# Six PSUM score banks as one tile with dependencies written out, and two subtractions of the row maximum in place of four

## The chip, the cores and the metric

The kernel runs on one core of a Trainium2 chip. Times are microseconds (us) of device time for one execution; the metric is the median of several executions. Engines: PE is TensorE (matmuls), PEld its weight load, DVE is VectorE, ACT is ScalarE, POOL is GpSimd, SP issues most DMAs. PSUM, where matmuls write, has eight banks of 512 float32 columns on 128 partitions.

## The reference, cut to what matters

Attention over pooled keys, followed by a soft mixture of experts. Keys and values are the same 768 pooled and projected rows a batch; there are 4 batches of 12288 queries of 128 channels.

```python
def _attn_ref(q, kv, w_sr):
    ...
    kv_pool = kv.reshape(B, H // r, r, W // r, r, C).mean(axis=(2, 4))
    kv_flat = kv_pool.reshape(B, -1, C) @ w_sr
    k = v = kv_flat
    s = scale * (q @ k.transpose(0, 2, 1))
    s = s - s.max(-1, keepdims=True)
    a = np.exp(s)
    a /= a.sum(-1, keepdims=True) + 1e-09
    return (a @ v).astype(np.float32)

def _moe_ref(x, phi, w1, w2):
    logits = x @ phi
    d = np.exp(logits - logits.max(0, keepdims=True)); d /= d.sum(0, keepdims=True) + 1e-09
    slot_input = d.T @ x
    ...
    c = np.exp(logits - logits.max(1, keepdims=True)); c /= c.sum(1, keepdims=True) + 1e-09
    return (c @ slot_out).astype(np.float32)
```

## The kernel before, in words

The queries are worked on in 96 blocks of 512. A block's scores are 6 tiles of 128 keys by 512 queries, one PSUM bank each, so six banks hold one block; the other two (`m0`, `m1`) serve everything else. The six are three PSUM tiles of two banks, with the tags s0, s1 and s2, allocated anew for every block.

For block i the steps are these. `qk(i, t)` (L553) makes score tile t with three matmuls, L560 to L562, high and low parts of keys and queries. `rowmax1` (L574) takes maxima over 32-query squares of two banks at once on DVE (L578); `rowmax2` (L588, L590) combines them, one small matmul on PE (`rowmax_pe`, L598) spreads them over the partitions, `rowmax3` (L603) reduces that and `rowmax4` (L608) transposes it into `mb`. `sub(i, t, n)` (L611) subtracts `mb` from n banks and writes to SBUF, into one of two tiles of three banks a block (L616). With a pair of banks a tile, four subtractions cover the six banks: banks 0 and 1, bank 2, bank 3, banks 4 and 5 (L1209). ACT makes two exponentials of each half (L624, L628), POOL their difference (`plo`, L633), and PE multiplies both parts by the values: `av_hi` (L650, L651) and `av_lo` (L658), four quarters of 128 queries a block. Every fourth block, a group of 2048 queries is worked into the experts' sums (`group_ops`, L1035), which adds smaller operations on all engines. The tail behind the last block runs the experts and writes the output; it uses the same six banks in pairs.

The order on PE, DVE, ACT and POOL is written out by the kernel's own planner (`Plan`, L37). Each operation has an engine, an assumed cost, a priority, operations that it depends on, and keys of buffer rings that it acquires or uses. The planner plays the program through with these costs and emits the instructions engine by engine in the order that results; the chip then runs each engine in that order. A ring entry is free again when its last user is done plus 0.08 us. A subtraction of n columns is assumed to cost n / 960 + 0.07 us. A block's first score matmul acquires ring s0, its third s1 and its fifth s2; the subtractions are among the users. For blocks below AHD = 10 the high part of the attention output may run before the low part of the exponentials is there; from block 10 on, its first piece also depends on `los`, POOL's low parts (L1164).

```python
for t, n in ((0, 2), (2, 1), (3, 1), (4, 2)):
    h, o2 = divmod(t, TH)
    ops["s", i, t] = op("DVE", dve(n * BQ), 0.08, ...)
```

Semaphores are set by the framework from the tiles that instructions touch. The first matmul into a newly allocated pair waits for the release of the pair's previous tile, that is for its last readers on DVE and for PE's own last writes.

Of the kernel before, what the change touches and what calls it, by code (L numbers as in the profile page):

```python
# [9 lines left out]
F32 = mybir.dt.float32  # L10
# [26 lines left out]
class Plan:  # L37
# [22 lines left out]
    def emit(self):  # L60
# [105 lines left out]
        while todo:  # L166
# [36 lines left out]
            fn()  # L203
        self.end = max(done)
# [3 lines left out]
def attention_then_soft_moe(ctx: ExitStack, tc: tile.TileContext, qT, kv0, kvT, w_sr, w_srT, phi, w1, w2, outT):  # L208
# [35 lines left out]
    TBUF = 3  # L244

# [66 lines left out]
    S = {}  # L312
# [9 lines left out]
    NU = NT // 2  # L322
# [3 lines left out]
        "pooled": 1, "v32": 1, "r6": 2, "rq": 2, "m1": 2, "mb": 1, **{f"s{u}": 1 for u in range(NU)},  # L326
# [3 lines left out]
    banks = [pm.tile([P, 512], F32, tag=f"m{b}", name=f"m{b}") for b in range(2)]  # L330

# [16 lines left out]
    WARM = (("s2", 2.2, 30, 0.32, 20.0), ("m", 26.3, 30, 0.22, 46.0))  # L348
# [215 lines left out]
    def qk0_hi(t):  # L564
        khi = kT[0][0]
        S[0, t // 2] = ps.tile([P, 2, BQ], F32, tag=f"s{t // 2}", name=f"s_0_{t // 2}")
        for u in range(2):
            for k in range(2):
                nc.tensor.matmul(S[0, t // 2][:, u, :], khi[:, (t + u) * P : (t + u + 1) * P], qsp[0][k], start=(k == 0), stop=False)

    def qk0_lo(t):
        nc.tensor.matmul(S[0, t // 2][:, t % 2, :], kT[0][1][:, t * P : (t + 1) * P], qsp[0][0], start=False, stop=True)

    def rowmax1(i, t, n):  # L574
        if t == 0:
            MX[i] = sp.tile([P, NT, NBK], F32, tag="r6", name=f"r6_{i}")
        u = t % 2
        nc.vector.tensor_reduce(  # L578
            out=MX[i][:, t : t + n, :].rearrange("p t b -> p (t b)"),
            in_=S[i, t // 2][:, u : u + n, :].rearrange("p t (b j) -> p (t b) j", j=Q32), axis=X,  # L580
# [30 lines left out]
    def sub(i, t, n):  # L611
        h, o = divmod(t, TH)
        if o == 0:
            TT_[i, h] = sp.tile([P, TH, BQ], F32, tag="t", name=f"t_{i}_{h}", bufs=TBUF)
        u = t % 2
        nc.vector.tensor_tensor(  # L616
            out=TT_[i, h][:, o : o + n, :], in0=S[i, t // 2][:, u : u + n, :],
# [18 lines left out]
    def av_tile(i, k):  # L636
        if k % 2 == 0 and i == NB - 1:
            PX[i, k // 2] = ps.tile([P, 2, BQ], F32, tag=f"s{k // 2}", name=f"px_{i}_{k}")[:, :, :VW]
# [323 lines left out]
    def warm(n, ring):  # L962
        if ring == "m":
            t = mt([P, 512], f"wm_{n}")
        elif n in W0:
            t = W0[n]
        else:
            t = W0[n] = ps.tile([P, 2, BQ], F32, tag=ring, name=f"wm_{n}")[:, 0, :]
# [145 lines left out]
    def av_rest(i, k, m, p, prev):  # L1114
        los = [ops["lo", i, 0], ops["lo", i, 1]]
        a2 = end_lo = op("PE", 6 * 0.072, 0.17, p + 0.8, prev + los, lambda: av_lo(i, k), use=[("plo", (i, 0)), ("plo", (i, 1)), m])
        if k % 2:
# [3 lines left out]
            if i == NB - 1:  # L1121
                v = k // 2
                q = HEAD + (i - 2) * PER + 0.01 * v
                a2 = op("DVE", 0.16, 0.08, q, [a2], lambda: l_x(v), use=[m], raw=0.05)
                a2 = op("DVE", 0.16, 0.08, q, [a2], lambda: l_r(v), raw=0.05)
                a2 = ops["l", v] = op("DVE", 0.24, 0.08, q, [a2], lambda: l_l(v), use=[m], raw=0.05)
            ops["x", i, k // 2] = op(
                "DVE" if i == NB - 2 and k == 1 else "ACT", act(2 * VW) + (0.1 if i == NB - 2 and k == 1 else -0.03), 0.1, p - 2, [a2] + evs[-1:], lambda: av_evac(i, k // 2),
                acq=[x] if first else [], use=[m] + ([] if first else [x]),
# [7 lines left out]
    def av_ops(i):  # L1137
# [7 lines left out]
        px = [(f"s{k // 2}" if end else "m", ("px", i, k // 2)) for k in range(TB)]  # L1145
        base = prev
        for k in range(TB if i < AHD else 0):
# [5 lines left out]
            for t in range(0, NT, AVS):  # L1153
                prev = [op("PE", 2 * AVS * 0.0702, 0.17, p, prev, lambda i=i, k=k, t=t: av_hi(i, k, t), acq=[m] if k % 2 == t == 0 else [], use=pp + ([m] if k % 2 or t else []))]
# [5 lines left out]
        for k in range(TB if i >= AHD else 0):  # L1160
            m = px[k]
            p = T0 + AVD * PER + 1.3 * k
            for t in range(0, NT, AVS):
                a1 = op("PE", 2 * AVS * 0.0702, 0.17, p, prev + ([] if end or t else los), lambda i=i, k=k, t=t: av_hi(i, k, t), acq=[m] if k % 2 == t == 0 else [], use=pp + ([m] if k % 2 or t else []))  # L1164
# [13 lines left out]
    for i in range(NB):  # L1178
# [8 lines left out]
        for t in range(NT):  # L1187
            u = t // 2
            if i == 0 and t == NT - 2:
                hi2 = op("PE", 4 * 0.2315, 0.0, T0 - QKP + 0.65 * t, [ops["ql", 0], ops["kh", 2], ops["qk", 0, t - 1]], lambda: qk0_hi(NT - 2), acq=[(f"s{u}", 0)], use=[("qs", 0)], raw=0.0)  # L1190
            ops["qk", i, t] = op(
                "PE", 0.2315, 0.17, T0 - QKP + 0.65 * t, [hi2] + kd + ([ops["qk", 0, t - 1]] if t == NT - 1 else []), lambda t=t: qk0_lo(t), use=[("qs", 0), (f"s{u}", 0)], raw=0.0,
# [407 lines left out]
```

## Time and profile before

| | before |
|---|---|
| median of 3 runs | 1063.73 us (1063.14 to 1064.67) |
| profiled execution, first to last instruction (its span; no other time of its own is listed) | 1063.4 us |
| PE busy | 1028.3 us, 97% |
| DVE busy | 972.7 us, 91% |
| POOL busy | 870.1 us, 82% |
| ACT busy | 794.1 us, 75% |
| DVE, row maxima L578 | 354.1 us, 289 instructions |
| DVE, subtractions L616 | 342.0 us, 384 instructions |
| mean granted TensorE clock | 0.990 |

An engine's busy time is the union of its instructions' spans. Matmuls overlap in the pipeline, so a matmul of 0.23 us may start 0.07 us behind the one before. A view of waits names the instruction that waited, what ended the wait, the total, how often, and the longest. A timeline lists instructions in order of start; neighbours of a kind are merged with a count (x2), the duration then reaching from the first start to the last end.

### The profile page before, as it was taken

To read this page: it belongs to the slowest core of one execution; us is meant where nothing else is said; L and a number is where in the kernel's file an instruction comes from. 1 tells how busy PE (TensorE), PEld (TensorE's weight loads), DVE (VectorE), ACT (ScalarE), POOL (GpSimd) and SP (SyncE) were. 2 spreads that over 40 slices of the span, in tenths; PEclk is the share of its full clock that TensorE was granted. 3 is DMA by queue.
4 is the path that set the end of the run, shared out by engine and by line. 5 is a ranking of instruction groups with operands and counts; after the bars stand their busy time and mean duration, and the time that the engine had idled before them with its cause. 6 is when DMAs were issued, how large, how long until landed. Compare 5 with 4: busy or idle time off the path is not lost.

```text
span 1063.4 us, 24815 instructions
## 1 busy us (share of the span) xinstructions
PE 1028.3 (97%) x10250; PEld 881.3 (83%) x10250; DVE 972.7 (91%) x1556; ACT 794.1 (75%) x1046; POOL 870.1 (82%) x505
## 2 busy tenths in 40 slices
PE   8999999999999999999999999999999999999894
PEld 5788888888888888988888888988888888888452
DVE  6989999999999999999999999999999999998684
ACT  3777787788777787788787787788787777776473
POOL 0789998889989989889989988889889999893800
PEclk9999999999999999999999999999999999999898
DMA  9234410120136320120146310120110110113598
GB/s 370 110 87 88 116 56 1 42 96 6 41 85 134 71 57 1 41 100 2 41 104 116 86 41 1 41 100 1 41 41 2 41 41 2 41 41 96 206 398 370
DMA packets 15729, 89.17 MB, mean 84 GB/s; under 512 B 1664, under 2 KB 1920, under 8 KB 9344
## 3 DMA queue, kind: packets, MB, share of 16 engines
q1 hardware_dynamic: 11728, 69.47, 17.6%
q0 software_dynamic: 3312, 17.70, 8.8%
q8 instruction: 81, 1.33, 0.5%
q10 hardware_dynamic: 576, 0.41, 0.1%
q14 instruction: 32, 0.26, 0.1%
HBM read 58.87 MB, written 25.17 MB: 79 GB/s over the span
## 4 chain that ended last, share of the span: by engine, by line
PE 87%; DVE 8%; DMA 3%; ACT 1%; issue 1%; POOL 0%; SPq 0%; DVEq 0%; ACTq 0%
PE m L650 15%; PE m L658 14%; PE m L651 14%; PE s L560 12%; PE s L562 11%; PE s L561 11%; PE m L831 2%; DVE r L578 2%; DVE t L616 2%; PE po L1429 2%; DMA outT<-o 2%; PE m L1401 1%; PE m L1407 1%; DMA kv<-kv 1%; DVE m L603 1%
## 5 line engine op out<-in xcount | busy, mean ns | idle before, releaser
L633 POOL TENSOR_TENSOR plo<-t,phi 128x1536 f16<-128x1536 f32 x190 | 599.2, 3164 | 93.1 <-ACT t L628 84.2
L624 ACT ACTIVATE phi<-t 128x1536 f16<-128x1536 f32 x192 | 283.5, 1478 | 148.1 <-DVE t L616 148.1
L578 DVE TRANSPOSE_TENSOR_REDUCE r<-s 128x32 f32<-128x1024 f32 x289 | 354.1, 1234 | 8.3 <-PE s L562 1.6
L650 PE MATMUL m<-vhi,phi 128*128 128x161 f16 x2280 | 353.2, 234 | 8.1 <-DVE m L603 7.3
L651 PE MATMUL m<-vlo,phi 128*128 128x160 f16 x2280 | 352.4, 233 | 0.0
L616 DVE TENSOR_TENSOR t<-s,mb 128x1024 f32<-128x1024 f32 (+1 forms) x384 | 342.0, 950 | 6.2
L628 ACT ACTIVATE t<-t 128x1536 f32<-128x1536 f32 x192 | 283.1, 1476 | 1.2
L650 PEld LDWEIGHTS <-phi 128*128 128x128 f16 x2304 | 224.1, 98 | 21.7 <-issue 21.5
L560 PE MATMUL s<-qhi,khi 128*128 128x512 f32 x574 | 237.1, 413 | 0.6 <-DVE t L616 0.4
L651 PEld LDWEIGHTS <-phi 128*128 128x128 f16 x2304 | 225.1, 98 | 12.1 <-issue 10.6
L562 PE MATMUL s<-qhi,klo 128*128 128x512 f32 x574 | 224.6, 391 | 0.0
L561 PE MATMUL s<-qlo,khi 128*128 128x512 f32 x574 | 223.9, 390 | 0.0
L658 PE MATMUL m<-vhi,plo 128*128 128x161 f16 x2280 | 223.5, 234 | 0.0
L658 PEld LDWEIGHTS <-plo 128*128 128x128 f16 x2304 | 171.9, 98 | 2.8 <-issue 2.7
L550 POOL TENSOR_TENSOR qlo<-q,qhi 128x512 fp32r<-128x512 f32 x95 | 127.9, 1346 | 23.9 <-ACT qhi L545 23.9
L562 PEld LDWEIGHTS s<-qhi,klo 128*128 128x128 f32 x574 | 107.7, 188 | 23.8
L560 PEld LDWEIGHTS s<-qhi,khi 128*128 128x128 f32 x574 | 107.9, 188 | 21.8 <-issue 2.6
L561 PEld LDWEIGHTS s<-qlo,khi 128*128 128x128 f32 x574 | 108.2, 189 | 19.4 <-issue 0.7
L668 ACT ACTIVATE xl<-m 128x322 f32<-128x322 f32 x189 | 81.4, 431 | 50.3 <-PE m L658 43.7
L608 DVE STREAM_TRANSPOSE mb<-m 128x512 f32<-128x512 f32 x96 | 68.3, 711 | 3.3
L545 ACT ACTIVATE qhi<-q 128x512 fp32r<-128x512 f32 x96 | 59.5, 620 | 2.8 <-DMA q<-qT 2.8
L603 DVE TENSOR_REDUCE m<-m 128x16 f32<-128x64 f32 x96 | 21.5, 224 | 22.8 <-PE m L598 19.1
(196 smaller groups left out, 843.3 us busy)
## 6 DMA issues: line engine op xcount, KB each, us to landing
q<-qT SPq DMA_DIRECT2D x23, 1024.0 KB, 5.0
outT<-o SPq DMA_DIRECT2D x22, 1024.0 KB, 7.6
kva<-kvT POOLq DMA_DIRECT2D x9, 1536.0 KB, 11.7
kva<-kvT SPq DMA_DIRECT2D x3, 1536.0 KB, 12.8
kv<-kv SPq DMA_DIRECT2D x6, 512.0 KB, 6.1
w<-w SPq DMA_DIRECT2D x2, 1536.0 KB, 6.4
w<-w SPq DMA_DIRECT2D x4, 768.0 KB, 4.2
kva<-kva POOLq DMA_DIRECT2D x3, 768.0 KB, 10.6
```

Source lines behind the costliest of these rows:

```text
L550: eng.tensor_tensor(out=lo, in0=q_src(i), in1=hi.bitcast(F32), op=ALU.subtract)
L560: nc.tensor.matmul(s, khi[:, ks], hi, start=True, stop=False)
L561: nc.tensor.matmul(s, khi[:, ks], lo, start=False, stop=False)
L562: nc.tensor.matmul(s, klo[:, ks], hi, start=False, stop=True)
L578: nc.vector.tensor_reduce(out=MX[i][:, t : t + n, :].rearrange("p t b -> p (t b)"), in_=S[i, t // 2][:, u : u + n, :].rearrange("p t (b j) ...
L616: nc.vector.tensor_tensor(out=TT_[i, h][:, o : o + n, :], in0=S[i, t // 2][:, u : u + n, :], in1=MX[i].unsqueeze(1).broadcast_to([P, n, BQ ...
L624: nc.scalar.activation(hi, TT_[i, h], AF.Exp, scale=SCALE)
L628: nc.scalar.activation(t, t, AF.Exp, scale=SCALE)
L633: eng.tensor_tensor(out=lo, in0=TT_.pop((i, h)), in1=PP[i, h][0], op=ALU.subtract)
L650: nc.tensor.matmul(px, p, vhi[:, t, :], start=(t == 0 and (i >= AHD or k % 2 == 0)), stop=False)
L651: nc.tensor.matmul(px[:, 1:], p, vlo[:, t, :], start=False, stop=False)
L658: nc.tensor.matmul(px, PP[i, t // TH][1][:, t % TH, ks], vhi[:, t, :], start=False, stop=(t == NT - 1 and (i >= AHD or k % 2 == 1)))
```

## The change

The three pair tiles become one PSUM tile `SB` of six banks that lives for the whole program. For the framework's tracking of this tile, a hook that runs after every planned operation puts orders between instructions on different engines bank by bank: an instruction waits, of the instructions on other engines that touched `SB`, only for the last one on each of its own banks (and for those that share another tensor with it). In the planner, the three rings of pairs become six rings of one bank; score tile t acquires ring t alone, and users of pairs name both banks. The subtraction runs over three banks at a time. The rest is renaming: the warm-up's bank, the last block's output, and the tail use slices of `SB`.

```diff
+    SUBS = ((0, 3), (3, 3))
...
-        "pooled": 1, ..., **{f"s{u}": 1 for u in range(NU)},
+        "pooled": 1, ..., **{f"s{t}": 1 for t in range(NT)},
...
+    SB = ps.tile([P, NT, BQ], F32, tag="s", name="s")
...
+    def order_banks():
+        for inst in seen:
+            if inst.opcode == "Ldweights":
+                continue
+            mine = banks_of(inst.outs) | banks_of(inst.ins)
+            if not mine:
+                continue
+            need = {x.name: x for b in mine for e, x in HELD.setdefault(b, {}).items() if e != inst.engine}
+            beside = others_of(inst)
+            for e, tensors in users.items():
+                if e != inst.engine:
+                    tc.declare_no_dep(
+                        inst, group=f"S{e}", keep=[x for x in need.values() if x.engine == e] + [x for n in beside for x in tensors.get(n, ())], reason="banks are waited for one by one"
+                    )
+            for n in beside:
+                users.setdefault(inst.engine, {}).setdefault(n, []).append(inst)
+            for n in need:
+                tc.add_manual_dep(inst, n, mybir.DependencyInfo(mybir.DependencyClass.Sync, mybir.DependencyReason.DATA), reason="same bank")
+            tc.add_to_no_dep_group(f"S{inst.engine}", inst)
+            for b in mine:
+                HELD[b][inst.engine] = inst
+        seen.clear()
...
     def qk(i, t):
-        if t % 2 == 0:
-            S[i, t // 2] = ps.tile([P, 2, BQ], F32, tag=f"s{t // 2}", name=f"s_{i}_{t // 2}")
-        s = S[i, t // 2][:, t % 2, :]
+        s = SB[:, t, :]
...
     def sub(i, t, n):
-        u = t % 2
         nc.vector.tensor_tensor(
-            out=TT_[i, h][:, o : o + n, :], in0=S[i, t // 2][:, u : u + n, :],
+            out=TT_[i, h][:, o : o + n, :], in0=SB[:, t : t + n, :],
...
-                lambda i=i, t=t: qk(i, t), acq=[(f"s{u}", i)] if t % 2 == 0 else [], use=[("qs", i)] + ([(f"s{u}", i)] if t % 2 else []),
+                lambda i=i, t=t: qk(i, t), acq=[(f"s{t}", i)], use=[("qs", i)],
...
-        for t, n in ((0, 2), (2, 1), (3, 1), (4, 2)):
+        for t, n in SUBS:
...
-                acq=[("t", (i, h))] if o2 == 0 else [], use=[(f"s{t // 2}", i), ("mb", i)] + ([("t", (i, h))] if o2 else []),
+                acq=[("t", (i, h))] if o2 == 0 else [], use=[(f"s{x}", i) for x in range(t, t + n)] + [("mb", i)] + ([("t", (i, h))] if o2 else []),
...
-    plan.emit()
+    nc.push_inst_callback(note)
+    plan.emit(order_banks)
+    nc.pop_inst_callback()
```

## Rows read from the trace of the kernel before

**Rows 1.** Busy us by engine, sum of the four 200 us stretches from 60 to 860:

```profile
sum 800.00, PE 791.74 PEld 700.24 DVE 758.09 ACT 629.50 POOL 721.83; mean PE 197.94 PEld 175.06 DVE 189.52 ACT 157.37 POOL 180.46
```

**Rows 2.** Who waited for whom: us in total, times, longest us:

```profile
ACT phi L624 <- DVE t L616: 148.1, 89, 2.8
...
DVE m L603 <- PE m L598: 19.1, 34, 0.9
...
PE m L650 <- DVE m L603: 7.3, 23, 0.3
```

**Rows 3.** Timeline of DVE, one block: start, duration, line, operation:

```profile
280.30 0.22 DVE L603 TENSOR_REDUCE m<-m 128x16 f32<-128x64 f32 x1
280.55 0.71 DVE L608 STREAM_TRANSPOSE mb<-m 128x512 f32<-128x512 f32 x1
...
281.30 1.22 DVE L616 TENSOR_TENSOR t<-s,mb 128x1024 f32<-128x1024 f32 x1
...
282.44 1.28 DVE L616 TENSOR_TENSOR t<-s,mb 128x512 f32<-128x512 f32 x2
...
283.04 1.81 DVE L616 TENSOR_TENSOR t<-s,mb 128x512 f32<-128x512 f32 x2
```

**Rows 4.** Timeline of PE and its weight loads, the same block:

```profile
280.06 0.20 PE L598 MATMUL m<-rq,sel_h 128*128 128x64 f16 x1
280.10 0.59 PE L658 MATMUL m<-vhi,plo 128*128 128x161 f16 x6
280.57 0.23 PE L650 MATMUL m<-vhi,phi 128*128 128x161 f16 x1
...
283.05 0.19 PEld L560 LDWEIGHTS s<-qhi,khi 128*128 128x128 f32 x1
```

**Rows 5.** Groups by shape on DVE: subtractions, busy us and mean ns:

```profile
L616 DVE TENSOR_TENSOR t<-s,mb 128x1024 f32<-128x1024 f32 x192 | 234.1, 1219 | 6.2
L616 DVE TENSOR_TENSOR t<-s,mb 128x512 f32<-128x512 f32 x192 | 123.1, 680 | 0.0
```

**Rows 6.** Timeline, second block's first weight load behind a subtraction:

```profile
27.99 1.22 DVE L616 TENSOR_TENSOR t<-s,mb 128x1024 f32<-128x1024 f32 x1
...
29.27 0.19 PEld L560 LDWEIGHTS s<-qhi,khi 128*128 128x128 f32 x1 [0.40 <-DVE t L616]
```

**Rows 7.** Timeline, an early block: subtraction, last matmul, weight load:

```profile
74.75 1.23 DVE L616 TENSOR_TENSOR t<-s,mb 128x1024 f32<-128x1024 f32 x1
...
75.84 0.23 PE L651 MATMUL m<-vlo,phi 128*128 128x160 f16 x1
...
76.12 0.47 PE L560 MATMUL s<-qhi,khi 128*128 128x512 f32 x1
...
76.09 0.19 PEld L560 LDWEIGHTS s<-qhi,khi 128*128 128x128 f32 x1 [0.23 <-issue]
```

**Rows 8.** Instructions of line L560: duration ns min/median/max, first and last start:

```profile
L560 PEldq EVENT_SEMAPHORE  x282: 51/51/51, 30.5 to 957.3; - x141
```

**Rows 9.** First subtraction and next score weight load: first and last of 46, then of 29:

```profile
131.55 1.22 DVE L616 TENSOR_TENSOR t<-s,mb 128x1024 f32<-128x1024 f32 x1
133.30 0.19 PEld L560 LDWEIGHTS s<-qhi,khi 128*128 128x128 f32 x1
...
943.51 1.22 DVE L616 TENSOR_TENSOR t<-s,mb 128x1024 f32<-128x1024 f32 x1
945.25 0.19 PEld L560 LDWEIGHTS s<-qhi,khi 128*128 128x128 f32 x1
...
122.21 1.23 DVE L616 TENSOR_TENSOR t<-s,mb 128x1024 f32<-128x1024 f32 x1
123.88 0.19 PEld L560 LDWEIGHTS s<-qhi,khi 128*128 128x128 f32 x1
...
952.93 1.23 DVE L616 TENSOR_TENSOR t<-s,mb 128x1024 f32<-128x1024 f32 x1
954.61 0.19 PEld L560 LDWEIGHTS s<-qhi,khi 128*128 128x128 f32 x1
```

More of the change, by code (lines that the diff above doesn't have):

```diff
@@ L58, in op, with emit @@
         return n
-    def emit(self):
+    def emit(self, after):
         ops = self.ops
@@ L203, in emit @@
             fn()
+            after()
         self.end = max(done)
@@ L311, in attention_then_soft_moe @@
     qsp = {}
-    S = {}
     MX = {}
@@ L321, in attention_then_soft_moe @@
     NBK = BQ // Q32
-    NU = NT // 2
     plan = Plan({
         "m": 2, "t": TBUF, "phi": PB, "plo": PB, "q": 2, "qs": 2, "xl": 2, "D": 1, "kv": 2,
-        "pooled": 1, "v32": 1, "r6": 2, "rq": 2, "m1": 2, "mb": 1, **{f"s{u}": 1 for u in range(NU)},
+        "pooled": 1, "v32": 1, "r6": 2, "rq": 2, "m1": 2, "mb": 1, **{f"s{t}": 1 for t in range(NT)},
     })
@@ L330, in attention_then_soft_moe, with note, others_of, banks_of @@
     banks = [pm.tile([P, 512], F32, tag=f"m{b}", name=f"m{b}") for b in range(2)]
+    SB = ps.tile([P, NT, BQ], F32, tag="s", name="s")
+    HELD = {}
+    seen = []
+    users = {}
+    def note(inst):
+        seen.append(inst)
+    def others_of(inst):
+        found = set()
+        for a in list(inst.outs) + list(inst.ins):
+            ap = getattr(a, "bass_ap", None)
+            if ap is not None and ap.tensor is not SB.tensor:
+                found.add(ap.tensor.name)
+        return found
+    def banks_of(args):
+        found = set()
+        for a in args:
+            ap = getattr(a, "bass_ap", None)
+            if ap is not None and ap.tensor is SB.tensor:
+                lo = ap.offset % (NT * BQ)
+                hi = lo + sum(s * (n - 1) for s, n in list(ap.ap)[1:])
+                found |= set(range(lo // BQ, hi // BQ + 1))
+        return found
+    def order_banks():
[20 more added lines that the diff above has]
+        seen.clear()
+    def pair(u):
+        return SB[:, 2 * u : 2 * u + 2, :]
+    def pr(u, key):
+        return [(f"s{2 * u}", key), (f"s{2 * u + 1}", key)]
     def mt(shape, name):
@@ L637, in av_tile @@
         if k % 2 == 0 and i == NB - 1:
-            PX[i, k // 2] = ps.tile([P, 2, BQ], F32, tag=f"s{k // 2}", name=f"px_{i}_{k}")[:, :, :VW]
+            PX[i, k // 2] = pair(k // 2)[:, :, :VW]
         elif k % 2 == 0:
@@ L1144, in av_ops @@
         end = i == NB - 1
-        px = [(f"s{k // 2}" if end else "m", ("px", i, k // 2)) for k in range(TB)]
+        px = [pr(k // 2, ("px", i, k // 2)) if end else [("m", ("px", i, k // 2))] for k in range(TB)]
         base = prev
@@ L1216, in attention_then_soft_moe @@
             t0 = t
-        se = {0: ops["s", i, 2], 1: ops["s", i, 4]}
+        se = {h: ops["s", i, max(t for t, n in SUBS if t < TH * (h + 1))] for h in range(NH)}
         for h in range(NH):
@@ L1301, in t_keep @@
     def t_keep():
-        W["ph1"] = ps.tile([P, 2, 512], F32, tag="s1", name="ph_0")
+        W["ph1"] = pair(1)
         W["ph", 0] = W["ph1"][:, 0, :]
@@ L1370, in t_busy @@
     def t_busy():
-        W["psq"] = ps.tile([P, 2, 512], F32, tag="s1", name="psq")[:, 0, :]
+        W["psq"] = SB[:, 2, :]
         for _ in range(SPAN):
@@ L1395, in c_t @@
             if g % 2 == 0:
-                U["t", g // 2] = ps.tile([P, 2, 512], F32, tag=f"s{2 - g}", name=f"pt_{g}")
+                U["t", g // 2] = pair(2 - g)
             pt = U["t", g // 2][:, g % 2, :]
@@ L1424, in o_mm @@
         for u in range(2):
-            U[g, "po", u] = ps.tile([P, 2, 512], F32, tag=f"s{(2 * g + u) % 3}", name=f"po_{g}_{u}")
+            U[g, "po", u] = pair((2 * g + u) % 3)
         for k, (a, c) in enumerate(((W["shi"], U[g, "hi"]), (W["shi"], U[g, "lo"]), (W["slo"], U[g, "hi"]))):
@@ L1525, in attention_then_soft_moe @@
                 m = sum(nt(x) for x in range(g, h))
[L1526 removed]
+                a = [x for y in range(g, h) for x in ops["ks", y]] + ([] if g else [ops["s", NB - 16, SUBS[-1][0]]])
                 a = op("ACT", act(m) + 0.1, 0.08, p, a, lambda g=g, m=m: k_add(g, m))
```

93 lines of the change are left out of this document (45 added, 48 removed).

## The prediction, made before the change was run

> **What bounds the kernel now.** I read the busy time by stretch first. In the four middle stretches of 200 us TensorE (PE) is busy for 791.7 of 800 us, VectorE (DVE) for 758.1 [rows 1]. Both look full, so the next view is who waits for whom. DVE waits 19.1 us for the small matmul of the row maximum (L598), and PE waits 7.3 us for the reduce behind it (L603) [rows 2]. DVE thus has idle time that PE causes, while PE has almost none; its largest wait is a round trip through DVE that no subtraction belongs to.
>
> The third view is the timeline of one block, because the change alters when score banks come free. PE's order of instructions is fixed by the planner. After L598 at 280.06 PE runs six low matmuls (L658), two further quarters of the attention output, and loads the weights of the next block's first score matmul (L560) at 283.05 [rows 4]. That is 2.99 us. Meanwhile DVE takes the answer of L598 (L603 at 280.30), transposes it (L608), and starts to subtract at 281.30, 1.24 us after L598 [rows 3, 4]. Its first subtraction, of banks 0 and 1, ends at 282.52. PE could therefore have had bank 0 half a microsecond before it asked for it. This slack of 0.5 us is what the change spends.
>
> **The change part by part.** (1) *Four subtractions become two.* A subtraction of 1024 columns takes 1.22 us and one of 512 takes 0.68 [rows 5], so 512 columns cost 0.54 and three banks should take 0.68 + 2 x 0.54 = 1.76 us. Back to back, the starts lie 1.14 us apart after 1024 columns (281.30 to 282.44) and 0.60 after 512 (to 283.04) [rows 3]: 0.06 us an instruction is fixed, since 2 x 0.60 - 1.14 = 0.06. Two instructions less save 0.11 to 0.12 us a block, 11 us of DVE over 96 blocks. I count this as nothing in the sum, because PE hides it: DVE ends earlier and then waits longer for the next L598. If that cover were gone it would be worth the whole 11 us (a rival below). ScalarE's exponentials start 0.06 us earlier in the first half (1.76 against 1.82) and 0.1 in the second; ScalarE waits 148.1 us for these subtractions in all [rows 2] and nothing on PE's path waits for it so soon, so this too is nothing.
>
> (2) *Bank 0 is given back later.* Before, 1.22 us after the subtraction's start; now 1.76, with banks 1 and 2. PE then loads weights either 0.05 us after the release (the second block: the subtraction ends at 29.21, the load starts at 29.27) [rows 6], or 0.11 us after it, where a separate semaphore instruction stands ahead of the load (ends at 75.98, load at 76.09) [rows 7]. So the load can start 1.81 or 1.87 us after the subtraction's start. Of the 85 blocks behind the first ten that have a successor, 46 load at 1.745 us, as the first and the last of them show, and 29 at 1.67, the DVE chain ahead of the subtraction being 0.07 us longer there [rows 9]; the other ten have more PE work in between and load at 1.81 or later. At 1.81 the sum is 46 x 0.065 + 29 x 0.14 = 3.0 + 4.1 = 7 us. At 1.87 it is 46 x 0.125 + 29 x 0.20 = 5.8 + 5.8 = 11.6 us. PE has no gap in which to make this up: its order stays as it is, and both its own work and DVE's chain up to the next L598 count from the start of the score matmuls, so each block is longer by the whole delay. Queued behind the waiting load are all of PE's matmuls; DVE's next row maxima wait for them.
>
> Does the planner see it? By its own costs bank 0 comes free 3.20 us after L598 (0.31 to reach the reduce, 0.23, 0.70 for the transpose, waits of 0.13, then 1.67 + 0.16), and PE arrives at 3.25, since it allows PE an idle 0.23 us for the row maximum that the trace hardly shows (L658 at 280.10, next quarter at 280.57 [rows 4]). It sees no wait, so it moves nothing. The chip's PE arrives at 2.99.
>
> (3) *Explicit dependencies instead of the tiles' own.* In the kernel before, the first matmul into each pair waits for DVE and for PE's own release of the tile; the second wait costs a semaphore instruction of 51 ns on PE's queue, 282 times, three in each of 94 blocks [rows 8]. With one lasting tile the release on PE itself should go, one wait remains, and I take the 0.05 us path, the nearest row with a single wait; 0.11 stays as the upper end. Banks 3 to 5 are released at about 3.44 and wanted at 1.81 + 3 x 0.68 = 3.85, so the second half costs nothing, with 0.4 us to spare. The row maxima still read pairs.
>
> (4) *The first ten blocks.* There PE already waits for bank 0: 0.28 us from the last matmul at 75.84 to the scores, some 0.2 more than a matmul takes [rows 7]. The release moves by 0.54. If all of it showed, nine blocks would lose 9 x 0.54 = 4.9 us; if it were filled completely, they would win 9 x 0.2 = 1.8. In these blocks the planner may put pieces of 0.28 us of the next block's attention output ahead of the scores (behind block ten it may not, as those wait for the low part first). I take nothing, since pieces of this size fill 0.54 almost exactly.
>
> (5) *Output stage, warm-up.* The tail's users of the banks still take pairs, the warm-up stays in the same bank, no DMA moves on SP's or POOL's queue. Nothing, within 1 us either way (an estimate: PE's 0.8 us of waits for the subtractions by the summary of waits is all that a finer order could give back).
>
> The sum is + 7 us. The profiled span is 1063.4 us, 0.3 below the median of 1063.73, so the forecast is 1063.7 + 7 = 1070.7; its own range is 1068 (less those 1.8 and 1) to 1077 (11.6 with 1.6 of the early blocks' 4.9).
>
> With this change PE waits for a DVE that has idle time of its own [rows 2], once in most blocks. The Trainium skill (Perfetto Trace Analysis, Optimizing Scalar/DVE Operations) says that where VectorE is not saturated but causes bubbles elsewhere, its instructions should be broken up so that work is finished sooner: by that rule this change goes the wrong way, as the rows also say.
>
> **The rivals.** *DVE sets the pace.* If the 95% of DVE were the bound in most blocks, every block would be shorter by 0.11 us: 1063.7 - 11 = 1053. For it: the small margin between the two engines; in blocks with group work on DVE the row maximum is late. Against it: the 19.1 us that DVE waits for L598 against PE's lack of idle time [rows 1, 2]. It decides if L598 waits for DVE by more than the new delay. Chance 0.20, including partial gains. The same page of the Trainium skill puts the fixed cost of a DVE instruction on PSUM at about 125 ns and says that grouping pays if the engine is saturated; by its figure this rival would be 192 x 0.125 = 24 us, an estimate that the 0.06 us of the timeline does not support.
>
> *The delay is covered.* Freed DVE time or another release time leads the planner to put other PE work between L598 and the scores in most blocks, as in the ten with slack. Then nothing shows: 1062 to 1065.5. For it: an order recomputed from changed costs; against it: its own 3.25 against 3.20, which leaves the order alone. Chance 0.17.
>
> *It does not do what it says.* If the single tile were still ordered as a whole, the scores would wait for both subtractions, until 3.44 + 0.05 = 3.49 us instead of 1.72: 75 x 1.77 = 133 us, so 1197. The code lifts exactly that order; chance 0.02.
>
> **How the numbers follow.** The forecast has 0.61. Its mechanism gives at least 4 us (7 less the 1.8 of the early blocks and the 1 of the tail), more than 0.2% (2.1 us), which is about what a measurement of this kernel can tell from no change. So slower is 0.61 + 0.02 = 0.63, same 0.17, faster 0.20. The range runs from 1077, the upper end of the forecast, down through the covered case to 1058, half of the DVE rival; what is left out is the rest of that rival and the whole-tile case.
>
> **What would show it.** Right: two subtractions of about 1.76 us; the score weights load 1.81 us after the first one's start in some 75 blocks, right behind its end; the line of waits from L560 to the subtraction grows from 0.8 us to several; DVE is busy for some 11 us less and waits longer for L598. Wrong: if other PE work stands between L598 and the scores, if the load follows the subtraction only by 0.11 us (then 1075), or if the blocks become shorter with PE's idle time unchanged, which would mean that DVE was the bound.

## The result, and the profile after

| | before | after |
|---|---|---|
| median (lowest to highest) | 1064.07 us (1063.14 to 1064.67) | 1079.6 us (1079.44 to 1080.15) |
| ratio, 95% interval | | 1.015 [1.0135, 1.0164] |
| span of the profiled execution | 1063.4 us | 1077.9 us |
| PE busy | 1028.3 us | 1035.5 us |
| DVE busy | 972.7 us | 972.1 us |

The kernel became 15.5 us slower. The forecast was 7 us slower, 1070.7, with a range to 1077: the sign was right and so was the mechanism inside the blocks, but about half of the loss came from behind the blocks, where the forecast had nothing.

In the listing of the changed kernel the lines have moved: the score matmul L560 is L615, the row maximum L578 is L631, L598 is L651, L603 L656, L608 L661, the subtraction L616 is L668, `plo` L633 is L685, the attention output L650, L651 and L658 is L702, L703 and L710, the router's L1366 and L1379 are L1418 and L1431, the output's L1429, L1436 and L1438 are L1481, L1488 and L1490. All six banks now have the one name `s`.

Busy time by engine, the sum of the same four 200 us stretches from 60 to 860 us as in [rows 1]:

```profile
sum 800.00, PE 791.10 PEld 696.84 DVE 748.85 ACT 627.87 POOL 713.21; mean PE 197.78 PEld 174.21 DVE 187.21 ACT 156.97 POOL 178.30
```

The 9.2 us that DVE has less than the 758.1 of before are not what the change saved: these stretches are equal in time, and the slower kernel does less work in one. On equal work, from the first subtraction of block 10 to that of block 95, the same view gives for the kernel before and then for the one after:

```profile
sum 840.63, PE 832.62 PEld 737.11 DVE 798.31 ACT 659.78 POOL 758.18; mean PE 832.62 PEld 737.11 DVE 798.31 ACT 659.78 POOL 758.18
...
sum 845.94, PE 837.33 PEld 738.38 DVE 793.07 ACT 660.56 POOL 754.20; mean PE 837.33 PEld 738.38 DVE 793.07 ACT 660.56 POOL 754.20
```

DVE is busy for 5.2 us less, and the stretch is 5.3 us longer. Of these, 4.7 us are counted as busy time of PE, though it has the same instructions to run. From the groups of instructions (busy us, mean ns, then idle us before them and what ended it), the row maxima of before and then two groups of after:

```profile
L578 DVE TRANSPOSE_TENSOR_REDUCE r<-s 128x32 f32<-128x1024 f32 x289 | 354.1, 1234 | 8.3 <-PE s L562 1.6 <-PE s L572 1.0
...
L631 DVE TRANSPOSE_TENSOR_REDUCE r<-s 128x32 f32<-128x1024 f32 x289 | 357.0, 1237 | 21.3 <-PE s L617 7.0
...
L668 DVE TENSOR_TENSOR t<-s,mb 128x1536 f32<-128x1536 f32 x192 | 328.7, 1752 | 6.0
```

A subtraction of three banks takes 1.75 us. The subtractions together are 13.3 us shorter than the 342.0 of before, and the idle time ahead of the row maxima is 13.0 us longer. The same block as in [rows 3, 4], DVE, PE and PE's weight load:

```profile
283.38 0.22 DVE L656 TENSOR_REDUCE m<-m 128x16 f32<-128x64 f32 x1
283.64 0.71 DVE L661 STREAM_TRANSPOSE mb<-m 128x512 f32<-128x512 f32 x1
284.39 3.42 DVE L668 TENSOR_TENSOR t<-s,mb 128x1536 f32<-128x1536 f32 x2
...
283.14 0.20 PE L651 MATMUL m<-rq,sel_h 128*128 128x64 f16 x1
...
286.20 0.19 PEld L615 LDWEIGHTS s<-qhi,khi 128*128 128x128 f32 x1
```

The weights of the next scores load 286.20 - 284.39 = 1.81 us after the first subtraction's start, 0.05 us behind its end; before, they loaded 1.75 us after it. From L651 to the load it is 3.06 us instead of 2.99. The view of the score line's waits (what its engine waited for: us, times) shows another part of the kernel:

```profile
L615 PEld LDWEIGHTS s<-qhi,khi x574: 186/188/191, 14.9 to 965.0; 128*128 128x128 f32 x192
...
  DVE t L668: 5.2, 11
```

Before it was 0.8 us in 3 waits. All 11 waits lie ahead of block 10, where PE now loads 1.81 us after the subtraction's start and before loaded after 1.34. From block 10 on the same view lists no wait for DVE: the delay there is 0.07 or 0.14 us a block, and it is seen in the starts of the loads alone. The separate semaphore instruction of [rows 8] has no row any more.

Where the 14.5 us of span lie is read off a few landmarks, the starts of single instructions in each trace: the first subtraction of block 10 and of block 95 (the last), the first matmul of the experts (L1305, now L1357), the first output matmul, and the end. The table has the time between landmarks, before, and by how much each kernel differs (the others are the experiments below).

| us | start to block 10 | block 10 to 95 | block 95 to the experts | experts to first output matmul | output to the end | sum |
|---|---|---|---|---|---|---|
| before | 122.21 | 840.63 | 19.40 | 13.26 | 67.90 | 1063.40 |
| after | +1.6 | +5.3 | +3.3 | +0.8 | +3.5 | +14.5 |
| a_copies | +1.3 | +5.6 | +3.2 | +1.0 | +0.8 | +11.9 |
| a_four | +1.9 | -0.3 | +0.5 | +0.8 | +4.0 | +6.8 |
| a_213 | +0.7 | +1.2 | +0.5 | +0.8 | +0.5 | +3.6 |
| a_early | +1.1 | +1.0 | +1.3 | +0.9 | -0.9 | +3.4 |
| b_rel_early | -0.3 | +0.3 | +3.4 | +0.9 | -0.9 | +3.5 |
| b_rel_late | +1.9 | +10.6 | +4.9 | +0.9 | -0.9 | +17.4 |
| b_tail | +1.2 | +7.1 | +2.0 | +0.2 | -0.4 | +10.2 |
| b_four | +1.7 | -0.1 | +0.5 | -0.3 | +0.5 | +2.4 |
| b_mix | -0.8 | +0.7 | +0.5 | -0.3 | -0.5 | -0.3 |

Each row is one execution, and executions of one kernel differ, at most by 4.1 us (b_four). One place where they do is the output: a_copies, b_rel_early and b_rel_late run the same instructions there, and it takes 1.7 us longer in a_copies. What differs with it is TensorE's granted clock in the first 15 us of the stage, for a_copies and then b_rel_early (windows: length, busy us of PE, PEld, DVE, ACT and POOL, the granted clock, then what the DMAs moved):

```profile
1006.55:1021.55 15.00, 12.07 (x87) 6.72 (x87) 9.35 (x14) 7.57 (x12) 9.42 (x11) 0.66 0.80 325
...
999.83:1014.83 15.00, 12.06 (x98) 7.10 (x102) 10.41 (x15) 8.79 (x14) 9.56 (x11) 0.77 0.79 323
```

The mean granted clock there is 0.66 in a_copies, a_213 and b_four, which stand at +0.5 to +0.8, and 0.77 in the kernel before and in the five kernels that stand at -0.4 to -0.9. So a difference of some 1.5 us in the output is not by itself the effect of an edit.

6.9 us come in the blocks, 5.3 of them from block 10 on, and 7.6 behind them, where the forecast had nothing. That the 6.9 lie so near to the 7 of the forecast is luck: it expected all of them from block 10 on and none before. Three things behind the blocks look different from before.

**Block 95 to the experts.** DVE and POOL before:

```profile
962.84 1.22 DVE L616 TENSOR_TENSOR t<-s,mb 128x1024 f32<-128x1024 f32 x1
963.99 0.15 DVE L782 TENSOR_REDUCE c<-m 128x1 f32<-128x4 f32 x1
...
964.90 0.17 DVE L792 TENSOR_TENSOR mrun<-mrun,m 128x32 f32<-128x32 f32 x1
...
968.27 1.75 DVE L633 TENSOR_TENSOR plo<-t,phi 128x1536 f16<-128x1536 f32 x1
970.91 0.27 DVE L698 TENSOR_SCALAR xl<-xl 128x12 f32<-128x12 f32 x1 [0.89 <-ACT xl L668]
...
971.47 0.23 DVE L682 TENSOR_SCALAR ru<-r,g 128x12 f32<-128x12 f32 x1
971.74 0.56 DVE L743 TENSOR_TENSOR LL<-xl,ru 128x384 f32<-128x384 f32 x1
...
972.49 1.75 DVE L633 TENSOR_TENSOR plo<-t,phi 128x1536 f16<-128x1536 f32 x1
...
965.21 1.28 POOL L797 TENSOR_TENSOR D<-LL,mrun 128x512 f32<-128x512 f32 x1 [0.49 <-DVE mrun L792]
```

and after:

```profile
969.73 3.42 DVE L668 TENSOR_TENSOR t<-s,mb 128x1536 f32<-128x1536 f32 x2
973.07 0.54 DVE L928 RECIPROCAL RM<-RM 128x64 f32<-128x64 f32 x1
973.69 0.16 DVE L834 TENSOR_REDUCE c<-m 128x1 f32<-128x4 f32 x1
...
974.75 0.18 DVE L844 TENSOR_TENSOR mrun<-mrun,m 128x32 f32<-128x32 f32 x1
974.85 2.51 DVE L685 TENSOR_TENSOR plo<-t,phi 128x1536 f16<-128x1536 f32 x1
977.69 2.19 DVE L685 TENSOR_TENSOR plo<-t,phi 128x1536 f16<-128x1536 f32 x1 [0.33 <-ACT t L680]
979.80 1.24 DVE L750 TENSOR_SCALAR xl<-xl 128x12 f32<-128x12 f32 x1
...
981.34 0.91 DVE L734 TENSOR_SCALAR ru<-r,g 128x12 f32<-128x12 f32 x1
982.28 1.36 DVE L795 TENSOR_TENSOR LL<-xl,ru 128x384 f32<-128x384 f32 x1
...
973.69 4.57 POOL L933 TENSOR_TENSOR LL<-LL,RM 128x512 f32<-128x512 f32 x3 [2.43 <-DVE RM L928]
978.23 2.78 POOL L849 TENSOR_TENSOR D<-LL,mrun 128x512 f32<-128x512 f32 x1
```

Before, the last group's small operations (L782 to L792, now L834 to L844) slip in between the pieces of the subtraction, 1.15 us after its start, and POOL goes on with them (L797) at 2.4 us. Now there are no pieces to slip between: they come behind both subtractions, at 4.0 us, and POOL's L849 starts at 8.5. A reciprocal (L876, now L928), which the planner lets run only where DVE has a hole, ran at 824.94 before; now it found no hole until 973.07, and three of its four multiplications on POOL (L933) stand ahead of L849. DVE's own order has changed too: before, the product L743 (now L795) ran ahead of the block's second L633, 8.9 us after the subtraction's start; now L795 comes behind both L685, at 12.6. The chain of work that ended last goes through DVE here, and four instructions of it are longer than before, while POOL works: the second L685 by 0.44 us, L750 by 0.97, L734 by 0.68 and L795 by 0.80.

**The router.** DVE waits for a matmul that it didn't wait for before:

```profile
1003.35 0.34 DVE L1420 TENSOR_SCALAR hs<-s,mask 128x128 f32<-128x128 f32 x1
1004.28 0.35 DVE L1418 SCALAR_TENSOR_TENSOR hs<-s,mask,hs 128x128 f32<-128x128 f32 x1 [0.58 <-PE s L1431]
```

L1418 writes one quarter of `hs` while L1431 reads another.

**The output copies.** DVE and ACT copy two halves of a group's output into one tensor `o`. Before, they start together (an early group of the output):

```profile
1001.17 1.23 DVE L1438 COPY o<-po 128x1024 f32<-128x1024 f32 x1 [0.85 <-PE po L1429]
1001.22 1.02 ACT L1436 ACTIVATE o<-po 128x1024 f32<-128x1024 f32 x1 [1.10 <-PE po L1429]
```

After, DVE starts when ACT is done, here and in the view of waits (us in total, times, longest us):

```profile
1010.59 1.02 ACT L1488 ACTIVATE o<-s 128x1024 f32<-128x1024 f32 x1 [0.59 <-PE s L1481]
1011.64 1.22 DVE L1490 COPY o<-s 128x1024 f32<-128x1024 f32 x1 [0.67 <-ACT o L1488]
...
DVE o L1490 <- ACT o L1488: 19.7, 23, 2.2
ACT o L1488 <- PE s L1481: 19.2, 22, 2.4
DVE m L656 <- PE m L651: 15.7, 38, 0.9
```

Both false orders have one source in the diff: `order_banks` lifts the framework's orders between two engines and keeps those of tensors that both touch by the tensor's *name*, without looking at which part of it.

### The profile page after: what moved, and what is told of

The parts are those of the page before. It is cut to its first block, busy times and chain, and to the rows that moved or that the text cites. A ratio compares the mean times of both kernels' runs of the same rounds, so it can differ in the third digit from the quotient of the medians.

```text
span 1077.9 us, 24188 instructions
## 1 busy us (share of the span) xinstructions
PE 1035.5 (96%) x10249; PEld 883.7 (82%) x10249; DVE 972.1 (90%) x1364; ACT 797.6 (74%) x1046; POOL 872.1 (81%) x505
## 4 chain that ended last, share of the span: by engine, by line
PE 90%; DVE 5%; ACT 2%; DMA 2%; issue 1%; SPq 0%; DVEq 0%; ACTq 0%
PE m L702 15%; PE m L710 15%; PE m L703 14%; PE s L615 13%; PE s L616 12%; PE s L617 12%; PE m L883 2%; PE s L1481 2%; ACT o L1488 1%; PE m L1453 1%; DVE t L668 1%; DVE o L1490 1%; DVE r L631 1%; DMA kv<-kv 1%; DMA outT<-o 1%
## 5 line engine op out<-in xcount | busy, mean ns | idle before, releaser
L685 POOL TENSOR_TENSOR plo<-t,phi 128x1536 f16<-128x1536 f32 x190 | 596.0, 3141 | 106.2 <-ACT t L680 91.1
L631 DVE TRANSPOSE_TENSOR_REDUCE r<-s 128x32 f32<-128x1024 f32 x289 | 357.0, 1237 | 21.3 <-PE s L617 7.0
L702 PE MATMUL m<-vhi,phi 128*128 128x161 f16 x2280 | 353.5, 234 | 10.5 <-DVE m L656 6.7
L703 PE MATMUL m<-vlo,phi 128*128 128x160 f16 x2280 | 352.8, 233 | 0.0
L668 DVE TENSOR_TENSOR t<-s,mb 128x1536 f32<-128x1536 f32 x192 | 328.7, 1752 | 6.0
L702 PEld LDWEIGHTS <-phi 128*128 128x128 f16 x2304 | 224.1, 98 | 21.7 <-issue 21.5
L615 PE MATMUL s<-qhi,khi 128*128 128x512 f32 x574 | 238.5, 416 | 1.6 <-DVE t L668 1.5
L703 PEld LDWEIGHTS <-phi 128*128 128x128 f16 x2304 | 225.1, 98 | 14.5 <-issue 13.1
L616 PE MATMUL s<-qlo,khi 128*128 128x512 f32 x574 | 224.3, 391 | 0.0
L710 PE MATMUL m<-vhi,plo 128*128 128x161 f16 x2280 | 223.2, 234 | 0.0
L710 PEld LDWEIGHTS <-plo 128*128 128x128 f16 x2304 | 172.4, 98 | 2.9 <-issue 2.8
L607 POOL TENSOR_TENSOR qlo<-q,qhi 128x512 fp32r<-128x512 f32 x95 | 125.7, 1323 | 24.1 <-ACT qhi L602 24.1
L615 PEld LDWEIGHTS s<-qhi,khi 128*128 128x128 f32 x574 | 107.7, 188 | 27.5 <-DVE t L668 3.7
L616 PEld LDWEIGHTS s<-qlo,khi 128*128 128x128 f32 x574 | 108.0, 188 | 19.1 <-issue 0.7
L661 DVE STREAM_TRANSPOSE mb<-m 128x512 f32<-128x512 f32 x96 | 68.3, 711 | 3.3
L1490 DVE COPY o<-s 128x1024 f32<-128x1024 f32 (+1 forms) x24 | 28.3, 1180 | 19.8 <-ACT o L1488 19.7
```

The costliest lines, as they stand in the source:

```text
L607: eng.tensor_tensor(out=lo, in0=q_src(i), in1=hi.bitcast(F32), op=ALU.subtract)
L615: nc.tensor.matmul(s, khi[:, ks], hi, start=True, stop=False)
L616: nc.tensor.matmul(s, khi[:, ks], lo, start=False, stop=False)
L631: nc.vector.tensor_reduce(out=MX[i][:, t : t + n, :].rearrange("p t b -> p (t b)"), in_=SB[:, t : t + n, :].rearrange("p t (b j) -> p (t b ...
L668: nc.vector.tensor_tensor(out=TT_[i, h][:, o : o + n, :], in0=SB[:, t : t + n, :], in1=MX[i].unsqueeze(1).broadcast_to([P, n, BQ]), op=ALU ...
L685: eng.tensor_tensor(out=lo, in0=TT_.pop((i, h)), in1=PP[i, h][0], op=ALU.subtract)
```

## The experiments

The theory after the result was: the blocks lose by the late release of bank 0, as forecast, and the output loses by the false order of the copies. Rival: the one tile with its hand-written order costs in every block, or the planner's new order does, whatever the release. Each run was compared with the kernel before on its chip, whose medians were 1063.5 to 1064.15 us.

**a_copies: the copies freed.** The change as it is, but the tensors `o_` are left out of the names that are kept.

```diff
-            if ap is not None and ap.tensor is not SB.tensor:
+            if ap is not None and ap.tensor is not SB.tensor and not ap.tensor.name.startswith("o_"):
```

> The changed kernel, but the output tiles (o_...) no longer count as a tensor that keeps an order between two users of the score tile; the two copies of a group, DVE's and ACT's, write different parts of it. Theory: in the output stage DVE's copy waits for ACT's copy of the same group (19.7 us of such waits), and that serial order costs the stage 3.4 us. Then DVE's copy starts together with ACT's, the stage from the first output matmul to the end is 67.9 us again instead of 71.3, and the total is 1079.6 - 3.5 = 1076, the block stage unchanged. Rival: the output stage is bound by its DMAs or by PE, DVE's wait is hidden: then 1079 to 1080.

Measured: 1076.41 us, ratio 1.0114 [1.0097, 1.0131]; 3.2 us less than the change, or 2.6 where each is taken against the kernel before on its chip. The stage behind the first output matmul is 68.75 us, 2.6 less than the 71.35 of the change, at the same mean granted clock (0.74 in the first 20 us of both). DVE no longer waits for ACT; what is left ahead of its copies are transfers and matmuls:

```profile
L1490 DVE COPY o<-s 128x1024 f32<-128x1024 f32 (+1 forms) x24 | 28.2, 1175 | 8.5 <-DMA outT<-o 5.3 <-PE s L1481 3.1
```

The false order of the copies is shown, and its price, 2.6 us. The stage is still 0.85 us longer than the 67.90 of before; that goes with the lower granted clock in the windows above.

**a_four: four subtractions again.** The change with the old cuts, the copies not freed.

```diff
-    SUBS = ((0, 3), (3, 3))
+    SUBS = ((0, 2), (2, 1), (3, 1), (4, 2))
```

> The changed kernel with the four subtractions of before: one tile, explicit dependencies, but bank 0 free after 1.22 us again. Theory (the late release of bank 0 costs the block stage its 6.9 us, the explicit dependencies cost nothing): the weights of the scores load 1.74 or 1.67 us after the first subtraction's start as before, the last block's subtraction starts within 1 us of 962.8, and the total is 1064 to 1068, by how much of the stages behind the blocks comes back. Rival (the dependencies or the per-bank rings cost the time, not the longer subtraction): 1075 or more, the last subtraction at 968 or later.

Measured: 1069.84 us, ratio 1.0061 [1.0046, 1.0076], 6.4 us above the kernel before on its chip; 9.2 us of the 15.5 are gone. It lies above what was expected, and the table of landmarks says why: from block 10 to 95 and on to the experts the loss is gone (-0.3 and +0.5), but the copies still wait (+4.0), and there is one hole in the ninth block, which the change itself doesn't have. There PE stands still for 1.97 us, since the planner put the group's 32 matmuls (L883) behind the first score bank instead of ahead of it:

```profile
113.63 0.58 PE L615 MATMUL s<-qhi,khi 128*128 128x512 f32 x1 [1.97 <-DVE t L668]
...
111.66:113.63 1.97, 0.00 (x2) 0.00 (x1) 1.87 (x3) 1.17 (x3) 1.97 (x2) 1.00 0.04 8
...
115.00:117.00 2.00, 2.00 (x34) 1.50 (x33) 1.06 (x2) 1.97 (x2) 1.80 (x2) 0.50 0.00 0
```

(The last two are windows: length, busy us of PE, PEld, DVE, ACT and POOL, then the granted clock of PE.) So most of the loss goes with the cuts, not with the dependencies.

**a_213 and a_early: three pieces, the first released early.** Both on top of a_copies.

```diff
-    SUBS = ((0, 3), (3, 3))
+    SUBS = ((0, 2), (2, 1), (3, 3))     # a_213
+    SUBS = ((0, 1), (1, 2), (3, 3))     # a_early
```

> As a_copies, with three subtractions: banks 0 and 1, bank 2, then banks 3 to 5. Bank 0 is free after 1.22 us, bank 3 after 3.49 as in the changed kernel. Theory: only the first release matters, so the block stage is as before (last subtraction within 1 us of 962.8) although DVE has one instruction less a block, and the total is 1063 to 1066. Rival (the long read of banks 3 to 5 delays something too, or DVE's saved 0.06 us a block comes through): over 1068, or 1060 and less.

> As a_copies, with three subtractions: bank 0 alone, banks 1 and 2, then banks 3 to 5. Bank 0 is free after 0.68 us. Theory: from block 10 on PE does not ask for bank 0 before 1.67 us, so nothing is won there; in the first ten blocks PE waits some 0.2 us a block for bank 0, which goes: 1 to 2 us less than a_213. Rival (an earlier release lets the planner reorder, or the gain is 0.06 us a block of DVE): over 5 us less than a_213, or more than a_213.

Measured: 1068.01 us, ratio 1.0042 [1.0026, 1.0057], and 1068.72, ratio 1.0045 [1.003, 1.006]. Both totals missed what was expected: a_213 takes 2 us more than the 1066 of its upper bound, 0.8 of them in the router, and a_early is not 1 to 2 us below a_213 but cannot be told from it (their runs overlap). From block 10 to 95 they lose 1.2 and 1.0 us, and no run shows why. The weights load at 1.742 us in the median block of both, as before the change, though a_early releases bank 0 at 0.69: half a microsecond of earlier release is worth nothing. So before the change PE did not wait for bank 0 in the median block. But cuts change two things at once, the release and the planner's order. The next two change only the release.

**b_rel_early and b_rel_late: the same order on every engine, another time of release.** On top of a_copies the planner still sees one subtraction of three banks, and only the code that it calls writes two instructions for it.

```diff
-        nc.vector.tensor_tensor(
+        for x, k in (((0, 2), (2, 1)) if t == 0 else ((0, n),)): nc.vector.tensor_tensor(   # b_rel_early
+        for x, k in (((2, 1), (0, 2)) if t == 0 else ((0, n),)): nc.vector.tensor_tensor(   # b_rel_late
...
```

> The kernel is the one with the copies freed (1076.4 us), with every engine's order of work kept as it is there; only the subtraction of banks 0 to 2 is written as two instructions, banks 0 and 1 first, then bank 2, so that banks 0 and 1 are released after 1.23 us and not after 1.76. Theory A, the time of the release costs the block stage its 5.6 us (block 10 to block 95: +1.28 to +6.84 us behind the kernel before): the score weights load again about 1.74 us after the first subtraction's start, the loss from block 10 to block 95 falls to under 1.5 us, and the whole takes about 1072 us. Theory B, the loss is the new order of the matmuls, which the planner wrote for one long subtraction: the loss stays at 4 to 6 us, and the whole stays at 1076 us. The stretch from the last subtraction to the experts stays as long as in the copies kernel (22.6 us) by both.

> As the run with the early release, with the two instructions the other way round: bank 2 first (0.61 us to the start of the next), then banks 0 and 1, so that bank 0 is released about 1.84 us after the first subtraction's start, 0.08 later than with one instruction. Theory A, the release sets the block: the weights load at about 1.89 us and not 1.81, every block from 10 on takes 0.08 us longer, 6 to 7 us in sum, so about 1083 us. Theory B, the order of the matmuls sets it: 1076 to 1078 us.

Measured: 1068.5 us, ratio 1.0048 [1.0033, 1.0063], and 1080.9, ratio 1.0162 [1.0145, 1.0179]. One block of each (the one shown of the kernel after), subtractions and the next weight load, early and then late:

```profile
282.01 3.49 DVE L668 TENSOR_TENSOR t<-s,mb 128x1024 f32<-128x1024 f32 x3
283.75 0.19 PEld L615 LDWEIGHTS s<-qhi,khi 128*128 128x128 f32 x1
```

```profile
285.87 3.49 DVE L668 TENSOR_TENSOR t<-s,mb 128x512 f32<-128x512 f32 x3
287.75 0.19 PEld L615 LDWEIGHTS s<-qhi,khi 128*128 128x128 f32 x1
```

The load stands at 1.74 and 1.88 us, against 1.81 with one instruction, and the stretch from block 10 to 95 loses 0.3, 10.6 and 5.6 us. With the order of work held the loss follows the release: theory A. Block by block, from the early release to the late one, 62 of the 85 blocks load later, all but one by 0.13 or 0.20 us, 9.95 in sum, and these 62 are 10.1 us longer; the other 23, where other work of PE stands ahead of the load, differ by 0.1 us in all. So the blocks that wait are longer by the whole delay, as the prediction had it. Both totals came out lower than expected, 1068.5 for 1072 and 1080.9 for 1083. In both the output took 1.7 us less than in a_copies; with the early release the first ten blocks gave 1.6 us more, and the late load is 0.063 us later than with one instruction (1.875 against 1.812), not 0.08. The first ten blocks go with the release too (-0.3 with the early one, +1.3 with one instruction, +1.9 with the late one). The stretch to the experts stays at +3.4, so that this one has another cause; the +4.9 of b_rel_late goes with a granted clock of 0.88 there, against 0.95 in b_rel_early.

**b_tail: the reciprocal no filler, `hs` by quarters.** On top of a_copies.

```diff
-                found.add(ap.tensor.name)
+                found |= {ap.tensor.name} if not ap.tensor.name.startswith("hs") else {...}   # one name for each quarter of 128 columns
...
-                joint = op("DVE", ..., lambda g=g, m=m: k_rec(g, m), fill=None if g else HEAD + (NB + 3) * PER)
+                joint = op("DVE", ..., lambda g=g, m=m: k_rec(g, m))
```

> The copies kernel (1076.4 us) with two edits behind the blocks. First, the reciprocal of the first join of groups (L928) is no filler any more, so that it needn't find a hole in VectorE's plan; it should run soon after its addition at 830 us, as in the kernel before (825), and not at 973. Second, the tensor hs is ordered by quarters and not as a whole. Theory C, the late reciprocal costs the stretch from the last subtraction to the experts 2.7 to 3.2 us, because its four multiplications on GpSimd then stand ahead of the last group's, and the hs order costs the router 0.6 us: that stretch falls from 22.6 to 19.4 to 19.9 us, the one from there to the first output matmul from 14.3 to 13.5, and the whole takes about 1073 us. Rival, the stretch is longer because the two second-half products on VectorE come late after a subtraction without pieces, whatever stands on GpSimd: 22 us or more, and 1075.5 to 1076.5.

Measured: 1074.69 us, ratio 1.0105 [1.009, 1.0121]. The order of `hs` did cost what was said: from the experts to the output the loss falls from 1.0 to 0.2 us. Of the reciprocal theory C was half right. It now runs at 831, and the stretch to the experts is 21.4 us instead of 22.6, where 19.4 to 19.9 was expected; and the blocks 78 to 95, where its multiplications now run, lose 1.6 us more, so that nothing is gained by this edit. The whole is 1.7 us less than a_copies, where 3.4 were expected, and it owes this to the router's 0.8 and to a shorter output (-0.4 against +0.8, at a granted clock of 0.77 against 0.66 in its first 15 us). The rival was right in part: L795 still stands behind both products, 11.3 us after the last subtraction's start. That left the places between the pieces for the rest.

**b_four: four subtractions, both false orders lifted.** a_four with the edits of a_copies and the `hs` edit of b_tail.

```diff
+    SUBS = ((0, 2), (2, 1), (3, 1), (4, 2))
```

> Four subtractions as before the change, the copies freed and hs ordered by quarters, so that of the change only the one tile with its order and the six rings of the plan are left. If what the four subtractions kept (6.8 us in the trace at the end) is the two false orders (3.9 us in the copies, 0.6 in the router) and one hole of 2.5 us in block 9, it takes about 1065.5 us: 1.4 to 3 us more than the kernel before. If the order by banks costs something in each block it stays at 1068 us or more.

Measured: 1065.44 us, ratio 1.0018 [1.0009, 1.0027], as expected. Its trace is 2.4 us behind, and the hole of block 9 alone is 2.5 (block 9 starts 0.8 us earlier than before, block 10 1.7 us later). Apart from this hole, the one tile with its hand-written order and the six rings cost nothing in the blocks.

**b_mix: all repairs together.** b_rel_early with `hs` by quarters, and with three pieces in the plan itself from block 78 on.

```diff
-    SUBS = ((0, 3), (3, 3))
+    SUBS, PIECES = ((0, 3), (3, 3)), 78
...
-        for t, n in SUBS:
+        for t, n in ((0, 2), (2, 1), (3, 3)) if i >= PIECES else SUBS:
```

> All repairs together: banks 0 to 2 subtracted in two instructions (banks 0 and 1 released early) under the plan made for one, the copies freed, hs ordered by quarters, and from block 78 on the plan itself made with three pieces, so that the reciprocal and the last group's small operations find places between them again. If the 15.5 us of the change are the late release (blocks), the lack of places between the pieces (last subtraction to experts), and the two false orders (router, output copies), and nothing else, then block 95 starts within 0.5 us of the kernel before (962.84 us), the stretch to the experts takes 19.4 to 20.0 us and not 22.8, the stretch from there to the first output matmul 13.0 to 13.5, and the whole takes 1064.3 us, within 0.2% of the kernel before. If the three planned pieces cost something in blocks 78 to 95, or the long stretch to the experts is not due to the pieces, it takes 1066 us or more. That one operation of VectorE fewer in each block brings nothing is expected by both.

Measured: 1065.01 us, ratio 1.001 [1.0001, 1.0019]; block 95 starts at 962.78 us and the stretch to the experts is 19.87. Its end of the blocks, to be read against the two above:

```profile
962.78 1.22 DVE L668 TENSOR_TENSOR t<-s,mb 128x1024 f32<-128x1024 f32 x1
963.92 0.15 DVE L834 TENSOR_REDUCE c<-m 128x1 f32<-128x4 f32 x1
...
964.83 0.17 DVE L844 TENSOR_TENSOR mrun<-mrun,m 128x32 f32<-128x32 f32 x1
...
968.20 1.75 DVE L685 TENSOR_TENSOR plo<-t,phi 128x1536 f16<-128x1536 f32 x1
970.81 0.18 DVE L750 TENSOR_SCALAR xl<-xl 128x12 f32<-128x12 f32 x1 [0.87 <-ACT xl L720]
...
965.14 1.28 POOL L849 TENSOR_TENSOR D<-LL,mrun 128x512 f32<-128x512 f32 x1 [0.70 <-DVE mrun L844]
...
968.72 2.13 POOL L864 TENSOR_TENSOR D<-D,rv 128x512 f32<-128x512 f32 x1 [2.09 <-ACT D L858]
```

The small operations are back between the pieces, L849 is back at 2.4 us, and the reciprocal runs at 824.7. With b_rel_early, which has the same three instructions in the last block but another plan, and takes 22.8 us, this shows that it is the plan's places that cost, not the instructions. The four repairs take back all of the 15.5 us but 0.9, and none of these kernels is faster than the one before: with one DVE instruction fewer in each block, b_mix is as fast as that within the 0.2% that can be told.

## Why the prediction was off

- **What bounds the kernel**: right. DVE is busy for 5.2 us less on the same blocks, and nothing is gained; in b_mix too.
- **(1) Two instructions saved, counted as nothing**: right as a term; a subtraction of three banks takes 1.75 us, forecast 1.76, and the subtractions are 13.3 us shorter in sum. Two of its signs were wrong. DVE is busy for only 0.6 us less in all, not 11: 5.2 less from block 10 to 95, and 4.6 more in the rest of the program. And the waits for L598 fell from 19.1 [rows 2] to 15.7 us; DVE waits for the next scores instead, with 21.3 us of idle time ahead of the row maxima (8.3 before).
- **(2) Bank 0 released later, +7 us**: right in place and kind, and too high in size. The load stands at 1.81 us, each block that waits is longer by the delay, and the stretch from block 10 on lost 5.3 us where 7 were forecast; in a_copies 5.3 of 5.6 go with the release (0.3 is left in b_rel_early). The 75 blocks of the sum were too many: 61 load later by 0.07 or 0.14 us, which makes 6.0, and in the other 14 the planner put more work of PE ahead of the load, so that it comes 0.23 or 0.25 us later, in b_rel_early as well. That "its order stays as it is" was thus wrong for PE too, though this new order costs nothing in sum.
- **(3) One wait instead of two, the 0.05 us path**: right; the load follows the subtraction by 0.05 us, the semaphore instruction is gone, and the uncut second half costs nothing (b_rel_early keeps it).
- **(4) First ten blocks, nothing**: too low; they lost 1.6 us, and b_rel_early, which loses none there, puts it down to the release. The bounds (-1.8 to 4.9) held it. With this term at 1.6 and term (2) at 5.3 the two errors nearly cancel.
- **(5) Output stage and warm-up, "nothing, within 1 us either way"**: this step failed. Behind the last block the change lost 7.6 us, and for 6.7 of it the runs show two reasons. The step looked at which banks the tail uses ("still take pairs") and not at what the new function does to every instruction that touches the tile: it keeps orders by tensor name, and so the copies (2.6 us, after against a_copies) and the router (0.8) got false ones. And the planner was examined only for PE's wait: it "sees no wait, so it moves nothing". It did move DVE's work. Small operations and a filler had lived in the places between the four subtractions, and with two uncut ones they went behind them, 3.3 us on the way to the experts, of which b_mix takes back 2.8. The last 0.9 us, in the output, stay in a_copies and not in b_rel_early, which runs the same instructions there at a higher granted clock.

Of the rivals, DVE as the pace is refuted by a_213 and b_mix, where fewer instructions with the old release bring nothing. The covered delay is refuted by b_rel_late, where the delay shows in full; the planner covered it in 14 blocks only. That the tile is still ordered as a whole is refuted by the load itself, 0.05 us behind the first subtraction. The sentence of the Trainium skill that the prediction weighed (Perfetto Trace Analysis, Optimizing Scalar/DVE Operations: where the engine isn't saturated but causes bubbles on others, breaking up instructions may let work be done sooner) agrees with these traces: the load goes back from 1.81 to 1.74 us with the three-bank subtraction in two, and on to 1.88 with the needed part last.

What stays open: why the output stage is 0.9 us shorter in a_early, b_rel_early and b_rel_late than in the kernel before, at the same granted clock of 0.77 in its first 15 us; why a_213 and a_early lose about 1 us from block 10 to 95; and why the reciprocal's multiplications cost 1.6 us in the blocks in b_tail and nothing in b_mix.

## What to carry to other kernels

Joining instructions on an engine that has idle time saved nothing here and gave back late what the first of them would have released; ask for each piece who waits for its end, and whether the slack is larger than the delay. Where a plan orders the work, the seams between pieces are also the places where small work goes: look for what lives there, on the joined engine too, up to the end of the kernel. When dependencies are written by hand, every instruction that touches the tile falls under the new rule, so compare the waits of stages that the edit doesn't name, above all where two engines write parts of one tensor.

## What the runs showed of the hardware

After PE had stood still for 1.97 us (a_four, 111.66 to 113.63), its granted clock was 0.60 in the mean up to 115.00 and 0.50, the lower of its two levels (1.2 GHz), up to 117.00, and score matmuls took 0.58 to 0.63 us instead of 0.40 to 0.47; in the kernel before, where the longest pause there was 0.77 us, the clock stayed at 1.00. From block 9 to block 10 it took 2.5 us longer than before, which is more than PE stood still.

Work of DVE and POOL at the same time made one or the other longer. In the trace after, the product L685 on DVE took 2.51 and 2.19 us beside POOL's L933 and L849, against 1.75 in b_mix, and L849 took 2.78 against 1.28; the small L750 took 1.24 against 0.18. But in b_mix L685 kept its 1.75 beside POOL's L864, which had started 0.52 us after it and took 2.13 instead of the 1.06 of its mean in the trace after. In each of these cases the one that grew had started second. The Trainium skill (SBUF — State Buffer, Who interferes with whom) says that the two engines share one pair of ports, and that this pair is an exclusive lock. The lengths fit that, but no run here measured it by itself.
